# First-layer gating as one VectorE operation, (tanh + 1) x values, with its power of two moved behind it

## The chip, the cores and the metric

The kernel runs on one core of one Trainium2 chip, as one program on its five engines: TensorE (PE, with its weight loads as PEld), VectorE (DVE), ScalarE (ACT), GpSimd (POOL) and SyncE (SP), which issues the DMAs. The metric is the device time of one execution in microseconds (us), the median of several runs. Lower is better.

## The reference, cut to what matters

```python
def _attn_ref(q, k, v):                      # B, H, S, D = 4, 8, 576, 64
    scores = (1 / np.sqrt(D)) * np.matmul(q, k.transpose(0, 1, 3, 2))
    kth = np.partition(scores, -32, axis=-1)[..., -32:-31]
    scores = np.where(scores >= kth, scores, -1e9)
    attn = np.exp(scores - np.max(scores, axis=-1, keepdims=True))
    attn = attn / (np.sum(attn, axis=-1, keepdims=True) + 1e-9)
    return np.matmul(attn, v)

def _moe_ref(x, w_gate, w_val, w_out):       # 2304 tokens, 512 -> 1536 -> 512
    gate = 1.0 / (1.0 + np.exp(-(x @ w_gate)))
    return (gate * (x @ w_val) @ w_out)

def _moe2_ref(x, w_in, w_out):               # 512 -> 2048 -> 512
    r = np.maximum(x @ w_in, 0.0)
    return (r * r) @ w_out

# attention, then its heads laid side by side as (2304, 512), then _moe_ref, then _moe2_ref
```

The gate is a sigmoid, which the kernel computes as (tanh(z / 2) + 1) / 2. The change concerns the product of this gate with `x @ w_val`.

## The kernel before, in words

The 2304 tokens are 18 tiles of 128. They go through the kernel in 12 chunks (`CHUNKS`, line 29): chunks 0 to 5 are one tile each (N = 128 columns), chunks 6 to 11 two tiles each (N = 256). Attention runs ahead of the two dense layers, one row block (a tile and a head) at a time: scores by matmul (L376) copied to an SBUF tile `S` (L379), four rounds of MAX8 and three of MATCH_REPLACE8 on VectorE over that tile (L392, L399) for the 32nd largest score, exponentials on ScalarE (L411, L413 or L427), scaling on ScalarE and GpSimd, a transpose by matmul or DMA, and the product with the values.

The weights are first converted and then split into a high and a low float16 part (`split`, L663 on ScalarE, L666 on VectorE, L668 and L669 on GpSimd); that work lies before 377 us. Chunks 0 and 1 (`moe32`) go through the layers in float32 and are not touched by the change. Chunks 2 to 11 use the split weights and also split each activation into two float16 parts, so that a product takes three matmuls (high x high, high x low, low x high).

The first layer of a chunk from 2 on goes in six pairs of 128-wide blocks of the hidden dimension, `fp` = 0 to 5. For one pair, `l1_pair` in `moe_head` (L744 to L770):

- 24 matmuls fill the PSUM tile `pg` (gate) and 24 more the PSUM tile `pv` (values), both at L753. `pg`, `pv` and the second layer's `ph` share one pool of two PSUM buffers, so the `pv` of the next pair can begin only when the VectorE operation that reads this pair's `pv` is done.
- ScalarE takes the tanh of `pg` into the SBUF tile `th` (L763).
- GpSimd makes (th + 1) x 2^(-TB-1) of it in place (L764; TB is 15).
- VectorE multiplies `pv` and `th` into `th` (L765).
- ScalarE rounds `th` to float16, the high part `gh[:, 0]` (L768).
- GpSimd subtracts: the low part `gh[:, 1]` = th - gh[:, 0] (L769).

The tiles are `gh` here, and `gp` for the first two pairs of chunks 5 to 11, which `start` begins while the chunk before them still runs. `l1_acc` (L793) then multiplies both parts with the split `w_out` and sums in PSUM, one pair or two pairs behind. After pair 5, the sum is scaled and split for the second layer (L823 to L834), which runs through L858 (`ph`), L867 to L871 and L879, and the tile goes out at L897.

The order of the instructions on every engine is not written by hand. The Tile framework's scheduler plays the program in a timeline of its own and puts each instruction where it becomes ready there, under priorities: attention has a high priority and is emitted ahead of the layers (`attend`, `at`). Each engine then executes its own list strictly in order, and a wait at its head holds everything behind it. So an edit of one operation can move other instructions in all lists.

A split product's first two matmuls per PSUM bank need only the high part; the third row of each accumulation needs the low part.

Of the kernel before, what the change touches and what calls it, by code (L numbers as in the profile page):

```python
# [14 lines left out]
AF = mybir.ActivationFunctionType  # L15
ALU = mybir.AluOpType
# [53 lines left out]
TB = 15  # L70
# [3 lines left out]
def tile_topk_attention__then__two_moe_layers(  # L74
# [14 lines left out]
    nc = tc.nc  # L89
# [599 lines left out]
    def wblk(name, a, kt, f0, n):  # L689
        t, e = parts[(name, kt, f0 // 512)]  # L690
        return t[:, a, e, f0 % 512 : f0 % 512 + n]
# [42 lines left out]
    def moe_head(ci, x):  # L734
        m = ahead[ci] = Moe()
        m.gp, m.queue = None, []
        tts = chunks[ci]
        N = len(tts) * P
        ig = scales["wg"][1]
        xs, ix = x  # L740
        gsc = xsmall[ci].bitcast(F32)[:, 4:5]
        nc.vector.scalar_tensor_tensor(gsc, ix, 0.5, ig, op0=ALU.mult, op1=ALU.mult)

        def l1_pair(fp, gh=None):  # L744
            pg = ps_w.tile([P, 512], F32, tag="wk", name=f"pg_{ci}_{fp}")
            pv = ps_w.tile([P, 512], F32, tag="wk", name=f"pv_{ci}_{fp}")
            for pp, wd in ((pg, "wg"), (pv, "wv")):
                for e in range(2):
                    f0 = (2 * fp + e) * P
                    n = 0  # L750
                    for c in range(KM):
                        for a, b_ in SPLIT:
                            nc.tensor.matmul(  # L753
                                pp[:, e * N : (e + 1) * N],
                                wblk(wd, a, c, f0, P),
                                xs[:, b_, c, :],
                                start=(e == 0 and n == 0),
                                stop=(n == 3 * KM - 1),
                                skip_group_check=True,
                            )  # L760
                            n += 1
            th = mpool.tile([P, 2 * N], F32, tag="hi", bufs=HIB, name=f"th_{ci}_{fp}")
            nc.scalar.activation(th, pg[:, 0 : 2 * N], AF.Tanh, scale=gsc)  # L763
            nc.gpsimd.tensor_scalar(th, th, 1.0, float(2.0 ** (-TB - 1)), op0=ALU.add, op1=ALU.mult)  # L764
            nc.vector.tensor_tensor(th, pv[:, 0 : 2 * N], th, op=ALU.mult)  # L765
            if gh is None:
                gh = mpool.tile([P, 2, 2 * N], F16, tag="hi", bufs=HIB, name=f"gh_{ci}_{fp}")
            nc.scalar.copy(gh[:, 0], th)  # L768
            nc.gpsimd.tensor_tensor(gh[:, 1], th, gh[:, 0], op=ALU.subtract)  # L769
            return gh  # L770

        m.N, m.ix, m.l1_pair = N, ix, l1_pair
# [517 lines left out]
```

## Time and profile before

| What | Value |
|---|---|
| Time, median of 3 runs | 1262.53 us (1261.23 to 1262.6) |
| Profiled execution, first to last instruction (span) | 1261.3 us |
| PE busy | 1176.1 us, 93% of the span, 11477 matmuls |
| PE weight loads | 957.5 us, 76% |
| VectorE busy | 954.8 us, 76% |
| GpSimd busy | 846.5 us, 67% |
| ScalarE busy | 828.6 us, 66% |
| Chain that ended last | PE 67%, ACT 9%, POOL 7%, DVE 7%, DMA 5%, issue 3% |

The three runs are the record of the time; the profiled execution is recorded by its span alone, 1.2 us under their median. Busy time on PE includes matmuls whose ends are modelled, so a stretch with 100% is one in which PE always had a matmul under way. An idle engine costs nothing unless the end waits for it: what matters is where PE stood still, and who released it.

### The profile page before, as it was taken

What the parts mean: (1) busy time and instruction counts of PE and PEld (TensorE: products, weight loads), DVE (VectorE), ACT (ScalarE), POOL (GpSimd) and SP (SyncE); (2) the same over time, 40 slices, a digit from 0 to 9 for tenths busy, and PEclk for the clock granted to TensorE, in tenths of its full rate; (3) what the DMA queues carried; (4) which work ended last, traced back from release to release, by engine and by line L of the source; (5) the groups of instructions that cost most, each with busy time, mean ns of one, the idle gap of its engine ahead of it and who ended that gap; (6) DMA issues with size and microseconds to landing.
All of it is one profiled execution on the core that took longest, in us unless ns stands there. A gap on an engine that the chain in (4) does not pass through costs nothing.

```text
span 1261.3 us, 30690 instructions
## 1 busy us (share of the span) xinstructions
PE 1176.1 (93%) x11477; PEld 957.5 (76%) x11477; DVE 954.8 (76%) x1965; ACT 828.6 (66%) x1719; POOL 846.5 (67%) x1294
## 2 busy tenths in 40 slices
PE   6757989999889998899998999999999999999998
PEld 5536877987777877779787778877876887787775
DVE  6998789899977978899988899999789969110010
ACT  4998996577767676677776777776567657322122
POOL 1788774488876577797876987797678659425223
PEclk9986999999989999999999999999999999999999
DMA  7988762223344356665776575567434523200000
GB/s 188 366 298 275 260 199 81 59 76 90 113 131 130 81 125 159 143 136 130 137 157 133 125 181 115 127 140 158 77 73 97 116 54 60 53 2 1 17 1 18
DMA packets 243190, 153.94 MB, mean 122 GB/s; under 512 B 193120, under 2 KB 209504, under 8 KB 243040
## 3 DMA queue, kind: packets, MB, share of 16 engines
q1 hardware_dynamic: 243040, 151.97, 47.7%
q8 instruction: 91, 1.49, 0.5%
q14 instruction: 59, 0.48, 0.1%
HBM read 105.51 MB, written 18.09 MB: 98 GB/s over the span
## 4 chain that ended last, share of the span: by engine, by line
PE 67%; ACT 9%; POOL 7%; DVE 7%; DMA 5%; issue 3%; SPq 2%; POOLq 0%; ACTq 0%; DVEq 0%
PE ph L858 12%; PE acc L879 12%; PE acc L793 8%; PE pg L753 8%; PE pv L753 8%; PE sp L376 5%; PE xp L509 3%; DMA PT<-S 3%; DVE mx L392 2%; PE xp L536 2%; DVE W L399 2%; PE pg L912 1%; PE qpt L336 1%; PE ph L959 1%; PE acc L976 1%
## 5 line engine op out<-in xcount | busy, mean ns | idle before, releaser
L392 DVE MAX8 mx<-W 128x8 f32<-128x576 f32 x432 | 327.9, 759 | 11.2
L399 DVE MATCH_REPLACE8 W<-mx,W 128x576 f32<-128x576 f32 x288 | 213.8, 742 | 0.0
L858 PE MATMUL ph<-x,wi_w 128*128 128x256 f16 (+1 forms) x1920 | 190.9, 253 | 2.7 <-ACT x L832 2.6
L879 PE MATMUL acc<-w_w,rh 128*128 128x512 f16 x768 | 182.2, 379 | 0.9 <-POOL rh L871 0.9
L858 PEld LDWEIGHTS <-wi_w 128*128 128x128 f16 x1920 | 156.4, 99 | 29.0 <-issue 4.0
L753 PE MATMUL pg<-xs,wg_w 128*128 128x256 f16 (+1 forms) x1440 | 148.4, 254 | 1.1 <-ACT th L763 0.8
L753 PE MATMUL pv<-xs,wv_w 128*128 128x256 f16 (+1 forms) x1440 | 143.8, 252 | 5.1 <-DVE th L765 3.7
L376 PE MATMUL sp<-kst,qt 128*128 128x288 f32 x608 | 132.9, 330 | 6.5 <-ACT rh L869 2.5
L457 POOL TENSOR_TENSOR S<-W,S 128x512 f16<-128x512 f32 x192 | 137.0, 735 | 2.1
L379 ACT COPY S<-sp 128x576 f32<-128x576 f32 x144 | 91.8, 638 | 66.3 <-PE sp L376 39.7
L793 PEld LDWEIGHTS <-wo_w 128*128 128x128 f16 x1440 | 119.6, 99 | 19.2 <-issue 7.4
L411 ACT ACTIVATE W<-S,mx 128x576 f32<-128x576 f32 x144 | 111.8, 776 | 30.9 <-DVE mx L392 30.5
L753 PEld LDWEIGHTS <-wg_w 128*128 128x128 f16 x1440 | 118.9, 99 | 17.2 <-issue 1.4
L753 PEld LDWEIGHTS <-wv_w 128*128 128x128 f16 x1440 | 117.4, 98 | 18.1 <-issue 5.8
L765 DVE TENSOR_TENSOR th<-pv,th 128x512 f32<-128x512 f32 (+1 forms) x60 | 34.7, 579 | 125.4 <-PE pv L753 121.0
L879 PEld LDWEIGHTS <-rh 128*128 128x128 f16 x768 | 72.0, 98 | 73.3 <-POOL rh L871 1.2
L392 DVE MAX8 mx<-S 128x8 f32<-128x576 f32 x144 | 107.3, 745 | 25.9 <-ACT S L379 24.1
L793 PE MATMUL acc<-gh,wo_w 128*128 128x256 f16 (+1 forms) x1104 | 105.6, 250 | 4.7 <-ACT gh L768 2.6
L399 DVE MATCH_REPLACE8 W<-mx,S 128x576 f32<-128x576 f32 x144 | 106.9, 742 | 0.0
L455 POOL TENSOR_SCALAR W<-W,bs 128x576 f32<-128x576 f32 x96 | 71.6, 746 | 52.6 <-ACT S L454 47.8
L870 POOL TENSOR_TENSOR r<-r 128x512 f32<-128x512 f32 (+1 forms) x80 | 69.6, 869 | 54.8 <-ACT rh L869 54.1
L376 PEld LDWEIGHTS sp<-kst,qt 128*128 128x128 f32 x608 | 90.8, 192 | 17.5 <-issue 3.8
(246 smaller groups left out, 2331.5 us busy)
## 6 DMA issues: line engine op xcount, KB each, us to landing
kst<-ks SPq DMA_DIRECT2D x112, 288.0 KB, 3.1
v<-vd SPq DMA_DIRECT2D x32, 320.0 KB, 3.3
qn<-in_q_dram SPq DMA_DIRECT2D x128, 64.0 KB, 2.3
wi_r<-in_moe_w_in_dram SPq DMA_DIRECT2D x16, 512.0 KB, 6.2
w_r<-in_moe_w_out_dram SPq DMA_DIRECT2D x16, 512.0 KB, 4.5
v<-in_v_dram SPq DMA_DIRECT2D x56, 128.0 KB, 2.4
wg_r<-in_moe_w_gate_dram SPq DMA_DIRECT2D x12, 512.0 KB, 6.0
wv_r<-in_moe_w_val_dram SPq DMA_DIRECT2D x12, 512.0 KB, 7.3
```

What stands on the lines that cost most here:

```text
L376: nc.tensor.matmul(sp[:, e, 0:HALF], l, r, start=(x == 0), stop=(x == len(ops) - 1))
L379: nc.scalar.copy(ss.rearrange("p (e s) -> p e s", e=2), sp[:, :, 0:HALF])
L392: m8 = nc.vector.max(mx[:, min(r, 1)], cur)
L399: nc.vector.match_replace(wk, mx[:, min(r, 1)], cur, NEG)
L411: nc.scalar.activation(wk, ss, AF.Prelu, bias=kth, scale=-1.0, alpha=1.0 / BIG)
L455: nc.gpsimd.tensor_scalar(wk, wk, rz, 1.0, op0=ALU.mult, op1=ALU.mult)
L457: nc.gpsimd.tensor_tensor(pp[:, o : o + e - f], wk[:, f:e], pp[:, f:e], op=ALU.subtract)
L753: nc.tensor.matmul(pp[:, e * N : (e + 1) * N], wblk(wd, a, c, f0, P), xs[:, b_, c, :], start=(e == 0 and n == 0), stop=(n == 3 * KM - 1), ...
L793: nc.tensor.matmul(accs[d // 2][:, (d % 2) * N : (d % 2 + 1) * N], wblk("wo", a, f, d * P, P), gh[:, b_, e * N : (e + 1) * N], start=(f == ...
L858: nc.tensor.matmul(ph[:, e * N : (e + 1) * N], wblk("wi", a, c, f0, P), x2[:, b_, c, :], start=(e == 0 and n == 0), stop=(n == 3 * KM - 1) ...
L870: nc.gpsimd.tensor_tensor(r, r, r, op=ALU.mult)
L879: nc.tensor.matmul(acc2[i][:, 0:DM], gh[:, b_, e * N + i * P : e * N + (i + 1) * P], wblk("w2", a, f, 0, DM), start=(f == 0 and x == 0), s ...
```

## The change

The factor 2^(-16) leaves the gate and goes behind the product. VectorE computes (th + 1) x pv in one operation, straight from the tanh. ScalarE's copy to float16 takes the factor as its scale, and GpSimd multiplies the float32 product by the same factor, in place, before it subtracts.

```diff
             th = mpool.tile([P, 2 * N], F32, tag="hi", bufs=HIB, name=f"th_{ci}_{fp}")
             nc.scalar.activation(th, pg[:, 0 : 2 * N], AF.Tanh, scale=gsc)
-            nc.gpsimd.tensor_scalar(th, th, 1.0, float(2.0 ** (-TB - 1)), op0=ALU.add, op1=ALU.mult)
-            nc.vector.tensor_tensor(th, pv[:, 0 : 2 * N], th, op=ALU.mult)
+            nc.vector.scalar_tensor_tensor(
+                th, th, 1.0, pv[:, 0 : 2 * N], op0=ALU.add, op1=ALU.mult
+            )
             if gh is None:
                 gh = mpool.tile([P, 2, 2 * N], F16, tag="hi", bufs=HIB, name=f"gh_{ci}_{fp}")
-            nc.scalar.copy(gh[:, 0], th)
+            nc.scalar.activation(gh[:, 0], th, AF.Copy, scale=float(2.0 ** (-TB - 1)))
+            nc.gpsimd.tensor_scalar(th, th, float(2.0 ** (-TB - 1)), 1.0, op0=ALU.mult, op1=ALU.mult)
             nc.gpsimd.tensor_tensor(gh[:, 1], th, gh[:, 0], op=ALU.subtract)
             return gh
```

In the changed kernel the VectorE operation is L764, the copy L769, the GpSimd multiplication L770 and the subtraction L771; every later line is two higher. The same number of operations is issued on each engine. Up to the first gating of chunk 2 the lists are the same; from there on they differ in many places. Three of them, all in chunk 2, follow. In a name such as `th_2_5_4241` the first number is the chunk, the second the pair, the last a buffer; `mx`, `W` and `S` tiles belong to attention (tile, then head), `w2_w` and `wi_w` to the weight split, and `x_3s`, `xt_3` and `xs_3` to the input of chunk 3.

VectorE, around the gating of pair 2 of chunk 2, before:

```order
L392 MAX mx_4_2_3821<-W_4_2_3820 128x8
L742 SCALAR_TENSOR_TENSOR x_3s_3573<-x_3s_3573,wsmall_89 128x1
L399 MATCH_REPLACE W_4_2_3820<-mx_4_2_3821,W_4_2_3820 128x576
L666 SCALAR_TENSOR_TENSOR w2_w4_3284<-w2_c4_1698,wsmall_89,w2_w4_3284 128x1024
L392 MAX mx_4_2_3821<-W_4_2_3820 128x8
L765 TENSOR_TENSOR th_2_2_3914<-pv_2_2_3865,th_2_2_3914 128x256
L392 MAX mx_4_3_4052<-S_4_3_3763 128x8
```

The same place in the changed kernel:

```order
L392 MAX mx_4_2_3821<-W_4_2_3820 128x8
L742 SCALAR_TENSOR_TENSOR x_3s_3573<-x_3s_3573,wsmall_89 128x1
L764 SCALAR_TENSOR_TENSOR th_2_2_3914<-th_2_2_3914,pv_2_2_3865 128x256
L399 MATCH_REPLACE W_4_2_3820<-mx_4_2_3821,W_4_2_3820 128x576
L666 SCALAR_TENSOR_TENSOR w2_w4_3284<-w2_c4_1698,wsmall_89,w2_w4_3284 128x1024
L392 MAX mx_4_2_3821<-W_4_2_3820 128x8
L764 SCALAR_TENSOR_TENSOR th_2_3_3995<-th_2_3_3995,pv_2_3_3946 128x256
```

The gating of pair 2 stands three large operations earlier, right behind L742, and that of pair 3 now comes before the first MAX of the next row block.

GpSimd, at the same pair, with what each instruction waits for, before:

```order
L224 TENSOR_TENSOR voe_1_0_3384<-ve_1_0_3380,voe_1_0_3384 64x2x64 [waits Pool_49]
L764 TENSOR_SCALAR th_2_2_3914<-th_2_2_3914 128x256 [waits Activation_49]
L716 TENSOR_SCALAR xt_3_2931<-xt_3_2931,x_3s_3573 128x512 [waits Activation_49]
L717 TENSOR_TENSOR xs_3_3566<-xt_3_2931,xs_3_3566 128x512 [waits PE_49,Pool_49]
L408 TENSOR_SCALAR bs_4_1_3694<-mx_4_1_3668 128x1
```

In the changed kernel:

```order
L224 TENSOR_TENSOR voe_1_0_3384<-ve_1_0_3380,voe_1_0_3384 64x2x64 [waits Pool_49]
L716 TENSOR_SCALAR xt_3_2931<-xt_3_2931,x_3s_3573 128x512 [waits Activation_49]
L770 TENSOR_SCALAR th_2_2_3914<-th_2_2_3914 128x256 [waits Activation_49]
L717 TENSOR_TENSOR xs_3_3566<-xt_3_2931,xs_3_3566 128x512 [waits PE_49,Pool_49]
L771 TENSOR_TENSOR gh_2_2_3917<-th_2_2_3914,gh_2_2_3917 128x256 [waits PE_49,Pool_49]
```

GpSimd's multiplication still waits for ScalarE, but now for the copy L769, which reads the tile that it overwrites; the subtraction behind it waits for GpSimd's own result and no longer for ScalarE.

GpSimd, at the last pair of chunk 2, before:

```order
L764 TENSOR_SCALAR th_2_5_4241<-th_2_5_4241 128x256 [waits Activation_49]
L408 TENSOR_SCALAR bs_4_4_4318<-mx_4_4_4310 128x1 [waits DVE_49]
L431 TENSOR_SCALAR bs_4_3_4078<-bs_4_3_4078 128x1 [waits Activation_49]
L220 MEMSET voe_1_2_4009 64x2x64 [waits DMAHW6_49,DMAHW4_49,Pool_49]
L431 TENSOR_SCALAR bs_4_4_4318<-bs_4_4_4318 128x1 [waits Activation_49,Pool_49]
L769 TENSOR_TENSOR gh_2_5_4245<-th_2_5_4241,gh_2_5_4245 128x256 [waits Activation_49]
```

In the changed kernel:

```order
L668 TENSOR_SCALAR w2_c6_1722<-w2_c6_1722,wsmall_89 128x1024 [waits Activation_49]
L770 TENSOR_SCALAR th_2_5_4241<-th_2_5_4241 128x256 [waits Activation_49]
L669 TENSOR_TENSOR w2_w6_3450<-w2_c6_1722,w2_w6_3450 128x1024 [waits Pool_49]
L771 TENSOR_TENSOR gh_2_5_4244<-th_2_5_4241,gh_2_5_4244 128x256 [waits PE_49,Pool_49]
L408 TENSOR_SCALAR bs_4_3_4078<-mx_4_3_4052 128x1
```

The four attention operations that stood between the two gating steps of this pair now stand behind them, and one of the weight split stands between. In PE's list, 24 matmuls lie between the last one of this pair's `pv` and the first that reads its `gh` before the change, and 56 after it.

## Rows read from the trace of the kernel before

**Rows 1.** Stretches, all engines: us, busy us (instructions) per engine, clock, DMA share, GB/s.

```profile
300.00:376.00 76.00, 66.87 (x795) 58.94 (x795) 67.01 (x134) 55.98 (x126) 59.20 (x90) 0.93 0.42 119
376.00:700.00 324.00, 303.81 (x3817) 257.01 (x3815) 282.37 (x631) 229.98 (x538) 237.76 (x435) 0.99 0.59 132
700.00:1090.00 390.00, 389.99 (x3719) 303.63 (x3714) 336.19 (x695) 265.37 (x551) 299.69 (x489) 1.00 0.52 110
```

**Rows 2.** Waits of PE, 300 to 700 us: us in total, times, longest.

```profile
PE kpt L164 <- DMA kn<-in_k_dram: 5.5, 3, 2.8
PE pv L753 <- DVE th L765: 3.7, 1, 3.7
PE acc L793 <- ACT gh L768: 2.6, 1, 2.6
PE sp L376 <- ACT rh L869: 2.5, 1, 2.5
...
PE acc L793 <- POOL gh L769: 2.0, 2, 1.6
```

**Rows 3.** Timeline of PE, chunk 2: start, us, operation, idle before and releaser.

```profile
335.24 1.50 PE L753 MATMUL pg<-xs,wg_w 128*128 128x128 f16 x24
340.45 2.06 PE L753 MATMUL pv<-xs,wv_w 128*128 128x128 f16 x24 [3.70 <-DVE th L765]
...
342.58 2.46 PE L753 MATMUL pg<-xs,wg_w 128*128 128x128 f16 x24
...
363.68 2.29 PE L793 MATMUL acc<-gh,wo_w 128*128 128x128 f16 x20 [1.55 <-POOL gh L769]
```

**Rows 4.** Stretches before and behind two stalls of PE, columns as in group 1.

```profile
335.00:340.40 5.40, 1.74 (x32) 1.62 (x30) 5.40 (x7) 1.37 (x2) 4.72 (x7) 1.00 0.29 70
340.40:345.00 4.60, 4.55 (x53) 4.53 (x53) 3.83 (x7) 4.60 (x14) 4.36 (x6) 0.63 0.04 9
361.50:366.00 4.50, 2.69 (x25) 2.53 (x25) 3.73 (x10) 1.18 (x5) 2.80 (x7) 0.52 0.59 145
```

**Rows 5.** Timeline of VectorE around the gating of pair 2, chunk 2.

```profile
334.32 2.20 DVE L742 SCALAR_TENSOR_TENSOR x_3s<-x_3s,wsmall 128x1 f32<-128x1 f32 x1
...
337.17 2.23 DVE L666 SCALAR_TENSOR_TENSOR w_w<-w_c,wsmall,w_w 128x1024 f16<-128x1024 f32 x1
339.32 0.75 DVE L392 MAX8 mx<-W 128x8 f32<-128x576 f32 x1
339.99 0.40 DVE L765 TENSOR_TENSOR th<-pv,th 128x256 f32<-128x256 f32 x1
```

**Rows 6.** Timeline of GpSimd, the same place.

```profile
336.00 0.40 POOL L764 TENSOR_SCALAR th<-th 128x256 f32<-128x256 f32 x1
...
337.17 1.15 POOL L717 TENSOR_TENSOR xs<-xt,xs 128x512 f16<-128x512 f32 x1
```

**Rows 7.** Groups by shape: busy us, mean ns of one, idle before.

```profile
L765 DVE TENSOR_TENSOR th<-pv,th 128x512 f32<-128x512 f32 x36 | 24.7, 687 | 121.9 <-PE pv L753 120.1 <-POOL th L764 1.2 <-POOL W L455 0.4
L833 DVE SCALAR_TENSOR_TENSOR x<-acc,x2s,x 128x512 f16<-128x512 f32 x12 | 8.6, 743 | 0.7 <-ACT x L832 0.6
L768 ACT CAST gh<-th 128x256 f16<-128x256 f32 x22 | 8.9, 406 | 2.8 <-DVE th L765 2.7
L869 ACT ACTIVATE rh<-r 128x256 f16<-128x256 f32 x32 | 13.4, 418 | 6.7 <-PE acc L879 3.2 <-POOL rh L871 3.1
L764 POOL TENSOR_SCALAR th<-th 128x256 f32<-128x256 f32 x24 | 9.7, 403 | 7.5 <-ACT th L763 7.5
L769 POOL TENSOR_TENSOR gh<-th,gh 128x256 f16<-128x256 f32 x22 | 15.1, 686 | 4.3 <-ACT gh L768 3.7
```

**Rows 8.** Timeline at the last pair of the last chunk.

```profile
1203.30 6.93 PE L793 MATMUL acc<-gh,wo_w 128*128 128x256 f16 x62
1203.57 0.69 DVE L765 TENSOR_TENSOR th<-pv,th 128x512 f32<-128x512 f32 x1 [7.17 <-PE pv L753]
...
1204.99 1.16 POOL L769 TENSOR_TENSOR gh<-th,gh 128x512 f16<-128x512 f32 x1 [2.72 <-ACT gh L768]
```

## The prediction

> **What bounds the kernel now.** I read four views, in this order. The stretches come first [rows 1]. From 700 to 1090 us PE is busy 389.99 of 390 us: there it is the bound, and nothing that happens on another engine can show in the time. From 376 to 700 us PE is busy 303.81 of 324 us (20.2 us idle) while VectorE is busy 282.37; from 300 to 376 us it is 66.87 of 76 (9.1 us idle), at a granted clock of 0.93. The kernel's matmuls are the same before and after, so the end moves by what PE's idle time before 700 us changes, and by what its clock loses there. Behind that the two layers of the last chunks are alone on PE; I come to their last gating below.
>
> The second view is who released PE between 300 and 700 us [rows 2]. Three of the lines belong to the gating: `pv` waits 3.7 us for VectorE's product L765, and `l1_acc` waits 2.6 us for ScalarE's copy L768 and 2.0 us for GpSimd's subtraction L769. They sum to 8.3 us. The timeline of PE [rows 3] puts them all into chunk 2's first layer: 3.70 us before 340.45, and up to 363.68 the two waits for the last pair, where PE reached `gh` early because only 24 matmuls lay between.
>
> The third view is the clock behind those stalls [rows 4]. PE worked at a granted clock of 1.00 up to the first stall and at 0.63 in the 4.6 us behind it; behind the second pair of stalls it was 0.52, that is almost all at the lower of its levels, 1.2 GHz, and not at 2.4. So a stall is paid for twice: 24 matmuls took 2.06 and 2.46 us behind it against 1.50 before, and 20 took 2.29 us, where 20/24 of 1.50 is 1.25 [rows 3]. That is 0.56 + 0.96 + 1.04 = 2.6 us.
>
> The fourth view explains the 3.70 us. VectorE's list had the product of pair 2 behind L742, a MATCH_REPLACE8, the weight split L666 (2.23 us) and a MAX8 [rows 5]; it began at 339.99. Its GpSimd input was done at 336.4 [rows 6] because GpSimd, in order, had been busy with the split of the attention values until 336.0. The scheduler had put the product late for the sake of that input.
>
> **The change, part by part.** *The GpSimd step leaves the path to the product.* That input is gone. In the new list the product of pair 2 stands right behind L742, which ended near 336.5, so it can end near 336.9 and not at 340.4. The `pv` of pair 3 then follows the `pg` that ended near 336.75 (335.24 + 1.50) with almost no gap: nearly all of the 3.70 us goes. What is late next is the low part of pair 2. The copy L769 can run from 337.0 to 337.4, the GpSimd multiplication (0.40) ends near 337.85, but L717 (1.15) stands between it and the subtraction (0.69), so the low part is there near 339.7. PE, with `pv` done at about 338.35, now goes straight to that pair's `l1_acc` and waits 1.35 us. I keep 1.35.
>
> *The step comes back behind the copy.* The words "beside that copy" do not hold: the multiplication writes `th` in place, so it waits for ScalarE's copy, as its wait in the list shows. The chain from product to low part becomes product, copy, multiplication, subtraction: 0.42 + 0.42 + 0.40 + 0.69 = 1.9 us for the narrow chunks, against 1.5 before [rows 7]. PE covers it wherever more work than this lies between: the smallest distance in the new list from a `pv` to the first matmul on its `gh` is 36 matmuls (pair 5 of chunk 3), or about 36 x 1.50 / 24 = 2.25 us. For the last pair of chunk 2 the distance grows from 24 to 56, about 3.5 us or more, and the four attention operations, two with a wait for ScalarE, no longer stand in GpSimd's gap; instead L669 does. I take 0.75 us as left of the 4.2 us there, halfway between none and the 1.55 us of the old wait for the subtraction.
>
> From chunk 5 on two pairs are under way, no distance in the new list is below 48 matmuls, and from 700 us on PE is full, so the longer chain is free. At the very end the low part of the last pair was ready at 1206.15 [rows 8]; 0.6 us more leaves it at 1206.8. On PE two earlier `l1_acc` of 24 matmuls each stand in front: 62 took 6.93 us, so 48 last from 1203.3 to 1208.7 [rows 8]. Free, with 1.9 us to spare.
>
> *VectorE's operation changes form.* It reads one tensor from SBUF and one from PSUM, as before. The nearest row of the same form and sources is L833, 743 ns at 512 columns against 687 for L765 [rows 7]; the other bound is no change. I take the upper one: +56 ns each, and less for the narrow ones. Of the 60 instances, those of chunks 2 to 6 lie where PE is not yet full: 30, at most 1.7 us of VectorE time. VectorE is 87% busy there (282.37 of 324 us [rows 1]), so I charge 1.0 us. The Trainium skill, "VectorE: DVE Perf Modes" (section "Why PSUM operands drop a tier"), holds any float32 operation with a PSUM operand to one result per cycle and makes no difference by form; by it this 1.0 us would be 0, and no row here shows this form with a float32 result.
>
> *ScalarE's copy gets a scale.* The nearest row is L869, an activation with a constant scale from SBUF to float16: 418 ns at 256 columns against 406 [rows 7]. That is +12 ns, 60 times, 0.7 us on an engine that is a third idle: 0.
>
> *GpSimd's work* is the same two operations a pair. What changes is that its list no longer stops at the tanh, only at the copy; attention operations behind it come earlier. I count nothing for it. No DMA is added or removed, though the order of some on SyncE's queue shifts.
>
> **The sum.** Removed: 8.3 us of stalls and 2.6 us of slow clock. Left or added: 1.35 + 0.75 + 1.0. Net 10.9 - 3.1 = 7.8 us by the end of chunk 2's first layer. Not all of this reaches 700 us. If attention comes forward as well, all of it does. If not, PE runs dry later, since the 20.2 us of idle time from 376 to 700 us is spent on waits such as 5.5 us for key loads and 2.5 us for `rh` [rows 2], which earlier layer work does not shorten. Between 0 and 7.8 I take half, 3.9, since VectorE, which paces attention, was itself not idle in the first stall (5.40 of 5.40 us [rows 4]) but lost 0.8 us in each of the two slow stretches. Against the median of 1262.5 (the profiled span is 1261.3, so the sum is of one execution 1.2 us shorter) that gives 1258.6 us.
>
> **The rivals.** *It only moves the idle time.* The lists differ in many places from chunk 2 on, and the net 7.8 us is used up by later waits. For it: attention work keeps its pace, and the scores of the next row blocks stand later among the layer's matmuls. Against it: PE is saturated later, so idle time once saved need not return. Time 1262, chance 0.24.
>
> *The longer chain is exposed, and it ends slower.* In chunks 3 and 4 the first layer runs one pair deep, with 36 to 107 matmuls of cover. ScalarE or GpSimd operations that stand in between (as L717 did with 1.15 us, or an L666-sized one with 2.2) push the low part past PE's arrival. The decisive point is a delay of more than about 0.4 us at the tightest pair (2.25 less 1.9) and 1.6 us at 56 matmuls (the first pair of chunk 4). Three such stalls of 2 us, each with 1 us of slow clock behind it (the 2.6 us came from three stalls), cost 9 us; less half of the 7.8 this is +5. Against it: the old chain, only 0.4 us shorter, stalled PE in chunk 2 alone. Time 1267, chance 0.26.
>
> *The new lists are better throughout.* All of the 7.8 us reaches the end, and a wait of 2.5 us elsewhere goes too: 1252. That is inside the forecast's direction, chance 0.12 of the 0.50 that I give to faster.
>
> **How the numbers follow.** 0.2% is 2.5 us, about what a measurement of this kernel can tell from no change. Faster by more: 0.50 (the forecast and the better case). Within: 0.24. Slower by more: 0.26. The range has to hold both signs: below, 7.8 us and one wait of 2.8 [rows 2] give 1252; above, the slower rival's 1267. Some tail beyond each is left out. The forecast's own range is 1254 to 1260.
>
> **What would show it.** Right: in the waits of PE, the line of `pv` for the VectorE operation is under 1 us, and those of `acc` for ScalarE and GpSimd are together under 3; the clock of 300 to 376 us is above 0.95; L764 takes 690 to 745 ns, L769 about 628, L770 617 at 512 columns; PE's idle time from 300 to 700 us falls from 29.3 to about 25. Wrong: `acc` waits for L771 in chunks 3 or 4, or waits for key loads and transposes grow by what the gating gave up.

## The result, and the profile after

The changed kernel is slower: 1272.59 us as the median of four runs (1268.48 to 1275.72) against 1262.57 us for the kernel before beside it, a ratio of 1.0088 with an interval of 1.0064 to 1.0112. The medians differ by 10.0 us, and the ratio is worth 11, where 4 us less were forecast; 1272.6 lies above the range. The profiled execution took 1272.85 us (span 1271.1). Ratios here and below are not the quotients of the two medians, from which they differ by up to 0.14%.

From the page of the changed kernel, busy times and the chain that ended last:

```profile
PE 1177.3 (93%) x11477; PEld 956.5 (75%) x11477; DVE 950.7 (75%) x1965; ACT 828.9 (65%) x1719; POOL 844.7 (66%) x1294
...
PE 61%; POOL 9%; DVE 8%; ACT 8%; DMA 8%; issue 4%; SPq 3%; POOLq 0%; ACTq 0%; DVEq 0%
```

No engine has noticeably more to do than before: PE's busy time grew by 1.2 us, VectorE's fell by 4.1. PE's part of the chain fell from 67% to 61%; DMA (5% before), GpSimd (7%) and VectorE (7%) took most of that over. The stretches of [rows 1], in the changed kernel (us, busy us and instructions of PE, PEld, DVE, ACT, POOL, granted clock, DMA share, GB/s):

```profile
300.00:376.00 76.00, 66.45 (x792) 56.86 (x791) 63.47 (x133) 57.51 (x127) 59.49 (x92) 0.98 0.39 110
376.00:700.00 324.00, 302.32 (x3757) 253.59 (x3755) 276.34 (x618) 222.39 (x528) 228.86 (x422) 0.97 0.59 132
700.00:1090.00 390.00, 387.97 (x3692) 302.76 (x3689) 342.91 (x710) 270.51 (x557) 305.56 (x498) 1.00 0.49 109
```

Three things differ from [rows 1]. The clock of the first stretch rose from 0.93 to 0.98, as forecast. That of the second fell from 0.99 to 0.97, and VectorE did 6 us less in it. And from 700 us on, where PE had been busy 389.99 of 390 us, it now stands still for 2 us. Who released PE between 300 and 700 us, to be held against [rows 2]:

```profile
PE sp L376 <- DMA kst<-ks: 6.6, 5, 1.7
PE kpt L164 <- DMA kn<-in_k_dram: 5.9, 3, 2.7
PE vn L214 <- ACT vs L205: 3.5, 2, 3.1
PE acc L881 <- POOL rh L873: 3.1, 2, 2.5
PE acc L795 <- POOL gh L771: 2.7, 2, 1.8
PE x2pq L827 <- ACT x L825: 2.7, 2, 1.5
PE xp L509 <- DMA PT<-S: 2.0, 2, 1.5
```

The 3.7 us of `pv` for VectorE's product are gone, and so are the 2.6 us of `acc` for ScalarE's copy. In their place stand waits that have nothing to do with the gating: key loads (`kst`), value norms (`vn`), the second layer's `rh`. For the transfers, the kernel before had:

```profile
PE sp L376 <- DMA kst<-ks: 1.7, 2, 1.0
PE xp L509 <- DMA PT<-S: 1.2, 2, 0.7
```

The gating itself, by shape (count, then busy us, mean ns of one, idle time of the engine before them):

```profile
L764 DVE SCALAR_TENSOR_TENSOR th<-th,pv 128x512 f32<-128x512 f32 x36 | 24.5, 681 | 117.8 <-PE pv L753 116.0 <-ACT W L411 1.3 <-ACT S L379 0.4
L764 DVE SCALAR_TENSOR_TENSOR th<-th,pv 128x256 f32<-128x256 f32 x24 | 9.9, 414 | 12.3 <-ACT th L763 7.9 <-PE pv L753 2.2 <-POOL gh L771 1.7
L769 ACT ACTIVATE gh<-th 128x512 f16<-128x512 f32 x24 | 15.0, 627 | 29.2 <-DVE th L764 29.2
L770 POOL TENSOR_SCALAR th<-th 128x512 f32<-128x512 f32 x36 | 22.2, 618 | 95.5 <-ACT gh L769 63.0 <-ACT gp L769 32.1 <-ACT vs L205 0.2
```

VectorE's new form takes 681 ns where the old product took 687 [rows 7]. So no operation of the gating got slower by more than 17 ns (ScalarE's copy of 256 columns, 406 ns before and 423 now), and the loss is to be looked for in what the rest of the program does around them.

### The profile page after: what moved, and what is told of

Read it like the earlier page. It is cut to its first block, busy times and chain, and to the rows that moved or that the text cites. A ratio compares the mean times of both kernels' runs of the same rounds, so it can differ in the third digit from the quotient of the medians.

```text
span 1271.1 us, 30671 instructions
## 1 busy us (share of the span) xinstructions
PE 1177.3 (93%) x11477; PEld 956.5 (75%) x11477; DVE 950.7 (75%) x1965; ACT 828.9 (65%) x1719; POOL 844.7 (66%) x1294
## 4 chain that ended last, share of the span: by engine, by line
PE 61%; POOL 9%; DVE 8%; ACT 8%; DMA 8%; issue 4%; SPq 3%; POOLq 0%; ACTq 0%; DVEq 0%
PE ph L860 10%; PE acc L881 9%; PE pg L753 8%; PE acc L795 8%; PE pv L753 7%; PE sp L376 5%; DVE mx L392 3%; PE xp L509 3%; DVE W L399 3%; DMA PT<-S 2%; PE xp L536 2%; DMA kst<-ks 2%; PE pg L914 1%; POOL S L457 1%; PE acc L936 1%
## 5 line engine op out<-in xcount | busy, mean ns | idle before, releaser
L764 DVE SCALAR_TENSOR_TENSOR th<-th,pv 128x512 f32<-128x512 f32 (+1 forms) x60 | 34.5, 575 | 130.1 <-PE pv L753 118.2
L795 PEld LDWEIGHTS <-wo_w 128*128 128x128 f16 x1440 | 117.0, 98 | 16.3 <-issue 4.0
```

What stands on the lines that cost most here:

```text
L795: nc.tensor.matmul(accs[d // 2][:, (d % 2) * N : (d % 2 + 1) * N], wblk("wo", a, f, d * P, P), gh[:, b_, e * N : (e + 1) * N], start=(f == ...
```

## Two theories, and how they were told apart

**The lists.** The change makes the scheduler draw new lists (the order of the instructions on each engine) from chunk 2 on, and these make PE wait more. **The operations.** The chain product, copy, multiplication, subtraction is longer and is exposed somewhere (the rival at 1267).

They can be separated, because an engine's order can be held. At the end of the program every instruction of an engine is chained to the one that is to stand ahead of it, by a dependency that is to set the order and add no wait (shortened; `lists` stands for the stored orders):

```diff
         tile_topk_attention__then__two_moe_layers(tc, *args)
+        pin(tc, nc)
...
+def pin(tc, nc):
+    at = {i.name: i for i in nc.cur_bb.bb.instructions}
+    for wanted in lists:
+        for earlier, later in zip(wanted, wanted[1:]):
+            tc.add_manual_dep(at[later], at[earlier].name, NOSYNC, reason="order")
```

`lists` holds the names of one engine's instructions in the order of either kernel; VectorE's product, ScalarE's copy and GpSimd's subtraction have a counterpart in both. GpSimd's fourth step (L764 before, L770 after) has none and finds its own place. In e1's trace PE, VectorE, ScalarE and SyncE run everything but the gating in the order of the kernel before, without one difference, and so does GpSimd but for four instructions at the start. Every kernel below computes the whole of the reference. Ratios are against runs of the kernel before on the same chip, whose medians were 1261.5 to 1262.7 us.

| Run | Operations | Lists | Median us | Ratio [interval] |
|---|---|---|---|---|
| e1 | changed | of before | 1263.74 | 1.0014 [1.0002, 1.0026] |
| e2 | before | of the changed kernel | 1272.78 | 1.0075 [1.0055, 1.0096] |
| e3 | changed | of before, gating free | 1266.24 | 1.0032 [1.0018, 1.0045] |
| e4 | before | of before (9 units in the first layers) | 1262.59 | 1.0000 [0.9987, 1.0012] |
| e5 | changed | its own | 1272.16 | 1.0088 [1.0062, 1.0115] |
| e6 | changed | new to 404 us, then of before | 1265.32 | 1.0031 [1.0019, 1.0043] |
| e7 | changed | of before to 404 us, then new | 1270.93 | 1.0067 [1.0047, 1.0088] |
| e8 | changed | new, SyncE's of before | 1287.80 | 1.0203 [1.0190, 1.0216] |
| e9 | changed | new, seven key loads earlier | 1274.38 | 1.0102 [1.0085, 1.0120] |
| e10 | changed | its own (9 units in the first layers) | 1272.93 | 1.0080 [1.0058, 1.0102] |
| e11 | changed | drawn anew, 13 units in the later layers | 1271.41 | 1.0078 [1.0061, 1.0094] |
| e12 | before | drawn anew, 13 units in the later layers | 1269.98 | 1.0057 [1.0035, 1.0079] |
| e13 | changed | of before to 700 us, then new | 1267.13 | 1.0039 [1.0025, 1.0052] |
| e14 | changed | new to 700 us, then of before | 1270.41 | 1.0048 [1.0032, 1.0064] |
| e15 | before | drawn anew, 15 units in the later layers | 1267.94 | 1.0042 [1.0026, 1.0058] |
| e16 | changed | drawn anew, 15 units in the later layers | 1266.80 | 1.0037 [1.0019, 1.0055] |

## Operations against lists: e1, e2, e3

e1, the changed operations with `lists` of the kernel before:

> The changed operations (VectorE (tanh+1) x values, ScalarE copy with the power of two, GpSimd multiplication right ahead of its subtraction), while every other instruction of all five engines is held in the order that it has in the kernel before; the product, the copy and the subtraction keep the places that they had there. Theory 1 (the loss comes from the new lists: the scheduler put attention work, weight splits and SyncE's transfers in another order, and PE waits more for key loads): 1260 to 1266 us, the waits for key loads and transposes as before (sp for kst about 2 us between 300 and 700, not 6.6). Theory 2 (the loss comes from the changed operations themselves: the longer chain product, copy, multiplication, subtraction): 1269 to 1275 us, with acc waiting for GpSimd more than the 2.0 us of before.

e2, the operations of before with `lists` of the changed kernel:

> The reverse: the operations of the kernel before, while every other instruction of all five engines is held in the order that it has in the changed kernel; only GpSimd's first step of the gating finds its own place. Theory 1: 1269 to 1277 us, with sp waiting for kst 5 us or more between 300 and 700. Theory 2: 1260 to 1266 us.

Measured: 1263.74 and 1272.78. The changed operations in the old lists cost 0.14% (1.8 us); the old operations in the new lists cost 0.75% (9.5 us). The theory of the lists holds in both directions, and the longer chain is worth at most the 0.26% at the end of e1's interval. In e1 PE's waits for the gating changed names rather than length (300 to 700 us):

```profile
PE xp L509 <- DMA PT<-S: 4.3, 5, 1.3
PE acc L795 <- ACT gh L769: 3.8, 2, 2.7
PE acc L795 <- POOL gh L771: 3.5, 4, 1.5
PE pv L753 <- DVE th L764: 2.1, 1, 2.1
...
PE sp L376 <- DMA kst<-ks: 0.7, 1, 0.7
```

That is 9.4 us for the three gating lines against 8.3 before [rows 2], while the key loads stay short. The transposes do not: they held PE for 4.3 us, against 1.2 before, which theory 1 had not expected.

e3 leaves the four gating operations out of `lists`, so that they alone may move forward, which is what the prediction counted on:

> As the first of these, but the four operations of the gating behind the tanh (product, copy, multiplication, subtraction) may move in their engines' lists; all else stands as in the kernel before. Theory 1: 1255 to 1262 us, the 3.7 us wait of pv for the product in chunk 2 gone and nothing new in its place. Theory 2: 1267 to 1275 us.

Measured: 1266.24, worse than e1 (1263.74) and between the two ranges, above that of the lists and just below that of the operations. The product of pair 2 of chunk 2 did move, from 339.99 [rows 5] to 335.87, and the wait of `pv` was gone. But PE stopped for 4.59 us in the same place. VectorE, ScalarE, GpSimd and PE there (start, us, operation, idle before and releaser):

```profile
335.87 0.41 DVE L764 SCALAR_TENSOR_TENSOR th<-th,pv 128x256 f32<-128x256 f32 x1
...
336.93 3.26 DVE L666 SCALAR_TENSOR_TENSOR w_w<-w_c,wsmall,w_w 128x1024 f16<-128x1024 f32 x1
...
340.23 1.15 ACT L663 ACTIVATE wi_w<-wi_c,wsmall 128x1024 f16<-128x1024 f32 x1 [3.50 <-DVE w_w L666]
...
342.56 0.45 ACT L763 ACTIVATE th<-pg,x_2s 128x256 f32<-128x256 f32 x1
...
336.96 0.39 POOL L770 TENSOR_SCALAR th<-th 128x256 f32<-128x256 f32 x1
337.33 1.15 POOL L717 TENSOR_TENSOR xs<-xt,xs 128x512 f16<-128x512 f32 x1
338.45 0.66 POOL L771 TENSOR_TENSOR gh<-th,gh 128x256 f16<-128x256 f32 x1
339.10 1.27 POOL L408 TENSOR_SCALAR bs<-mx 128x1 f32<-128x1 f32 x1
...
343.07 2.72 PE L753 MATMUL pg<-xs,wg_w 128*128 128x128 f16 x24 [4.59 <-ACT th L763]
```

ScalarE's list has a copy of the weight split (L663) ahead of the next pair's tanh, and that copy waits for VectorE's split L666, which here took 3.26 us and 2.23 in [rows 5]. The `pg` of the pair behind waits for the buffer that this tanh reads. In the kernel before that tanh was done at 342.53, just ahead of the `pg` that began at 342.58 [rows 3]:

```profile
342.06 0.47 ACT L763 ACTIVATE th<-pg,x_2s 128x256 f32<-128x256 f32 x1
```

So the 3.7 us were never the product's alone: beside them stood a second chain, VectorE's split to ScalarE's copy to the tanh, that left no room.

## Is any new set of lists a loss? e4, e10, e11, e12, e15, e16

The scheduler was to draw anew without a change of any operation, by the number of units that attention runs ahead: 10 in the first layers (`LEAD`), 14 in the later ones (`LEAD2`).

```diff
-LEAD = 10
+LEAD = 9
```

> The kernel before with one number of the order changed (how many units attention runs ahead in the first layers, 9 and not 10): no operation differs, only the lists from chunk 2 on. Theory 1: such a change of the lists alone moves the time by 2.5 us or more, in either direction (1250 to 1260 or 1265 to 1275). Theory 2 says nothing of it but a change of the lists alone should matter little: 1260 to 1265.

> The changed kernel with attention 9 and not 10 units ahead in the first layers: the scheduler draws its lists anew for the same operations. If the loss is one unlucky set of lists, not a property of these operations: 1262 to 1268. If any lists that the scheduler makes for these operations lose: 1269 to 1276.

```diff
-LEAD2 = 14
+LEAD2 = 13
```

> The changed kernel with attention 13 and not 14 units ahead in the later layers. As for the run with 9: 1262 to 1268 if the lists were unlucky, 1269 to 1276 if any lists for these operations lose.

> The kernel before with 13 and not 14 units: no operation differs. If lists drawn anew cost some tenths of a per cent whatever the operations, since those of the kernel before are the best of several: 1265 to 1275. If its scheduler's lists are as good for any such number: 1260 to 1264.

```diff
-LEAD2 = 14
+LEAD2 = 15
```

> The kernel before with attention 15 and not 14 units ahead in the later layers; no operation differs. If the lists of the kernel before are a favourable draw among neighbours (13 units cost 0.57%): 1266 to 1275. If 13 was the exception: 1260 to 1264.

> The changed kernel with 15 and not 14 units. If the changed operations have some favourable set of lists near by, as the kernel before has with 14: 1258 to 1266. If they lose with every number near by (13 units gave 1271.4, 14 units 1272): 1268 to 1276.

The number for the first layers redrew nothing. In e4's trace VectorE, ScalarE, GpSimd and SyncE run the same lines on the same tiles and shapes in the same order as in the kernel before, from first to last, and PE differs in four matmuls near 36 us; e10 stands to the changed kernel in the same way. (Traces leave buffer numbers out, so that a swap of two operations alike in all this would not show.) So e4 and e10 are repeats, at 1262.59 and 1272.93, and say nothing about new lists; what e4's theory 1 expected of a redrawing was not put to the test by it. The number for the later layers does redraw: e12 leaves the lists of before at 592 us and e15 at 488, e11 and e16 leave those of the changed kernel at about 490.

With 13 units the old operations take 1269.98 and the changed ones 1271.41; with 15, 1267.94 and 1266.80. So at the two neighbouring numbers old and new operations differ by +0.21% (0.78 less 0.57, each uncertain by some 0.2) and -0.05%: nothing that these runs can tell from no change. Only at 14 do they differ by 0.88%. (e16 fell between its two expectations, with single runs from 1259.5 to 1272.4; e10 and e11 fell into the one of a loss. It is e12 and e15 that show that a loss does not need the changed operations.) The kernel before has favourable lists at that number, and each of the five other sets that were tried (the changed kernel's, e11, e12, e15, e16), whether its cause was a number or an operation, cost 0.37 to 0.88%. Five are few, and three of them share their first 490 us. With e1 and e2 that is the answer to why a change that removed its stalls came out slower.

## Where the new lists lose: e5 to e9, e13, e14

The changed kernel once more, unedited:

> The changed kernel once more, for a second profile. It is to show how much of the difference ahead of 316 us is its own: the lists are those of the kernel before up to there, yet its first profile stood 1.9 us later at the first matmul of chunk 2 and had 4.6 us more of idle PE. If that belongs to one execution, this profile stands within 0.5 us of the kernel before at that matmul and still ends at 1270 to 1274; if it belongs to the kernel, it is 1.5 us late again.

It ended at 1272.16, and its first matmul of chunk 2 came 2.9 us late, where the first profile had 1.9; both have lower clock around 175 us, but so has e11, which came 0.3 us late. Three others with new lists (e2, e9, e10) were within 0.4 us there and still took 1272.8 to 1274.4. That early loss is therefore not what makes the difference; what causes it in those two profiles stays open.

Four cuts change lists at one moment: every engine follows the one kernel's list up to it, and takes what is left in the order of the other.

> The changed operations; every list is held as in the changed kernel up to the end of chunk 2 (404 us) and behind that as in the kernel before. If the new lists gain in chunk 2 (its second layer begins 4 us earlier there) and lose only behind it: 1257 to 1262. If the gain in chunk 2 is attention's loss, to be paid later whatever follows: 1264 to 1270. If the changed operations cost what is lost: 1269 to 1275.

> The changed operations; every list as in the kernel before up to 404 us, and as in the changed kernel behind that. If the loss sits behind chunk 2: 1268 to 1274. If it sits in chunk 2: 1262 to 1266.

> The changed operations; every list as in the kernel before up to 700 us and as in the changed kernel behind that. The prediction held that from 700 us on nothing on another engine can show, since PE was busy 389.99 of 390 us there: then 1262 to 1265, like the changed operations in the lists of before (1263.7). If the new lists let PE run dry there by themselves: 1266 to 1271.

> The reverse cut: lists of the changed kernel up to 700 us, those of the kernel before behind that. If the loss is made by 700 us, as attention's delay of 10 us at row block 88 says, and is only collected later: 1269 to 1274. If it is made behind 700 us: 1263 to 1267.

Of the runs with changed operations, e1 has none of the new lists (0.14%). New lists up to 404 us bring e6 to 0.31%, from 404 to 700 as well e14 to 0.48%; behind 700 us alone they bring e13 to 0.39%. So the three pieces cost 0.17, 0.17 and 0.25%, with the operations 0.73% in sum (9.2 us) against 0.88 measured for the whole. Each difference is uncertain by about 0.2%, so that only the last is clear of zero, and the pieces cannot be ranked: by medians the second is the largest (4.2 us, against 1.4 and 2.3). e7 gives the lists behind 404 us directly: 0.67 less 0.14, or 0.53%. For e6 and e7 the second and the first expectation held (1264 to 1270, 1268 to 1274). The cut at 700 us was to tell on which side of it the loss is made, and both sides came out with one: 1267.13 is in e13's range for PE running dry by itself, 1270.41 in e14's for a loss made by 700 us. So neither side has all of it.

The loss can be followed in attention's progress, one row block (tile and head) after the other. Start of the first MAX8 of a block, and how much later it starts in the other profiles (us):

```
block  before     e1     e6    e13     e9  after    e12
   40   390.5    0.7    0.5    0.0    1.3    1.9   -1.0
   56   499.7    1.9    2.3   -0.5    3.0    7.1   -0.8
   72   604.6    2.9    2.9    1.5    6.2   10.0    0.4
   88   712.2    3.5    3.1    6.5   11.9   12.9    3.0
  104   812.9    4.3    3.8    9.8   14.4   15.7    9.4
  112   858.7    4.1    3.6   12.5   17.5   17.9   11.5
  143  1070.9    3.8    3.5    5.1    8.7    9.5    6.0
```

In the changed kernel attention falls 18 us behind, and about half of that is left at the end. e6 shows that what chunk 2 gains does not last: its second layer began 5.8 us earlier than before, and by chunk 3's second layer it was 1.7 us late. Presumably the first layer had gone ahead of attention's matmuls, which then had to be made up. e12 shows the same fall behind with no operation changed, and late: from block 72 on, as its lists change only at 592 us. Delay and loss do not go in step, though: at block 112 e16 is 14.4 us late and e15 2.1, and their last chunks begin 5.0 and 2.1 us late. That attention's delay is the cause is not shown; no run moves attention alone.

In e13 all lists are old up to 700 us, and still PE runs dry behind that, by its waits from 700 to 930 us and the stretch (columns as above):

```profile
PE xp L509 <- DMA PT<-S: 1.7, 2, 1.1
PE sp L376 <- DMA kst<-ks: 1.0, 1, 1.0
```

```profile
700.00:930.00 230.00, 227.17 (x2240) 179.38 (x2239) 201.74 (x424) 157.89 (x336) 177.34 (x302) 1.00 0.58 126
```

In the kernel before PE was busy 229.99 us of these 230. So with other lists a late transpose or key load stopped PE even in its fullest stretch.

Whether SyncE's transfers do it was tried twice. e8 takes `lists` of the changed kernel for four engines and that of the kernel before for SyncE:

> The changed operations and the changed kernel's lists on PE, VectorE, ScalarE and GpSimd; only SyncE's list of transfers is that of the kernel before. If the loss comes from the place of the key loads in SyncE's list (kst behind the stores of value pieces): the waits of sp for kst fall from 6.6 us to under 3 and the time to 1263 to 1267. If the order on the compute engines sets when keys can be loaded: the waits stay or move to other loads, 1270 to 1276.

1287.8 us, far above both expectations, with 12.5 us of waits for `kst` from 300 us on. SyncE's old list, which serves the old lists of the others, does not fit these new ones. e9 moves only seven key loads, each ahead of the transpose behind which the new list had put it. The place of one of them, SyncE's queue in the changed kernel:

```profile
476.42 1.32 SPq L459 DMA_TRANSPOSE PT<-S  x1
...
481.46 2.10 SPq L328 DMA_DIRECT2D kst<-ks  x2
```

and in e9:

```profile
470.25 0.62 SPq L328 DMA_DIRECT2D kst<-ks  x1
473.08 1.32 SPq L459 DMA_TRANSPOSE PT<-S  x1
```

> The changed kernel with its own lists but for one thing: in SyncE's list seven of the 112 key loads (kst), which stand there behind one transpose more than in the kernel before, stand ahead of that transpose again. If key loads behind a transpose that waits for attention are what carries the loss: the waits of sp for kst fall from 7 to 8 us to under 4, attention's row block 56 starts 2 us or more earlier, and the time is 1263 to 1268. If they are only one of many places at which the new lists wait: 1268 to 1273.

The local effect came: waits of `sp` for `kst` between 300 and 700 us fell from 6.6 to 3.6 us, and block 56 started 3.0 us late, not 7.1. The time did not follow (1274.38). By block 88 attention was 11.9 us late again. That fits the second expectation, by which key loads behind transposes are one of many places, although the time lies above its range too.

PE's side of the account, by stretches in the kernel before:

```profile
316.00:404.00 88.00, 78.75 (x1015) 67.72 (x1014) 72.17 (x149) 62.79 (x147) 66.46 (x110) 0.94 0.44 122
404.00:700.00 296.00, 275.92 (x3489) 235.80 (x3487) 262.34 (x589) 210.60 (x489) 217.80 (x395) 0.99 0.60 133
700.00:930.00 230.00, 229.99 (x2267) 182.69 (x2262) 205.70 (x431) 160.60 (x341) 179.14 (x303) 1.00 0.58 127
```

and in the changed kernel:

```profile
316.00:404.00 88.00, 77.88 (x998) 65.55 (x998) 67.90 (x148) 63.60 (x149) 66.67 (x112) 0.98 0.43 122
404.00:700.00 296.00, 274.89 (x3442) 232.99 (x3443) 256.89 (x577) 203.70 (x480) 208.90 (x383) 0.97 0.59 131
700.00:930.00 230.00, 227.97 (x2249) 180.23 (x2247) 204.76 (x429) 162.18 (x343) 182.53 (x309) 1.00 0.56 127
```

PE's idle time grows by 0.87, 1.03 and 2.02 us, 3.9 in sum. As an estimate, the clock takes (1 - clock) x length: 5.3 us before and 1.8 after in the first stretch, 3.0 and 8.9 in the second, net 2.4 us, uncertain by some 2 since the clock has two digits. That accounts for 6.3 of the 7.9 us by which the first profile fell back between chunk 2's first matmul and the last chunk's (1.9 to 9.8 us late). The second profile of the same kernel, e5, divides the loss otherwise:

```profile
316.00:404.00 88.00, 78.40 (x976) 65.72 (x976) 67.94 (x147) 63.98 (x148) 67.84 (x113) 0.94 0.44 120
404.00:700.00 296.00, 276.20 (x3487) 234.14 (x3485) 260.08 (x584) 206.83 (x484) 211.27 (x386) 0.98 0.59 132
700.00:930.00 230.00, 224.79 (x2186) 176.70 (x2185) 200.40 (x416) 156.78 (x332) 178.41 (x300) 0.99 0.57 126
```

There PE's idle time grows by 0.35, -0.28 and 5.20 us, and the clock by the same estimate takes 0, 3.0 and 2.3 us more: 10.5 us, where this profile fell back by 10.0 (2.9 to 12.9 us late). So the clock gave back in chunk 2 what the forecast said (3.5 us against 2.6) in one profile and nothing in the other. What both share is a loss behind 404 us, by this estimate 9 to 10 us of idle time and slow clock together.

## Why the prediction was wrong, point by point

*The removed stalls: right.* The wait of `pv` was to fall under 1 us and fell to 0; those of `acc` for ScalarE and GpSimd were to be under 3 us in sum and were 2.7; the clock from 300 to 376 us was to be above 0.95 and was 0.98. In e5, the second profile, the stalls are gone too, but that clock was 0.93, as before the change.

*PE's idle time: wrong.* From 300 to 700 us it was to fall from 29.3 to about 25 us, and rose to 31.2 (29.4 in e5). The sign named for a wrong prediction came instead: waits for key loads and transposes grew by 5.7 us (1.7 to 6.6 and 1.2 to 2.0), about the 5.6 that the gating gave up (8.3 to 2.7).

*What is left of the gating: right in kind, off in size.* PE at the two places in the changed kernel and behind the second, and GpSimd between multiplication and subtraction of either pair:

```profile
340.94 1.22 PE L795 MATMUL acc<-gh,wo_w 128*128 128x128 f16 x19 [0.92 <-POOL gh L771]
...
360.23 1.39 PE L795 MATMUL acc<-gh,wo_w 128*128 128x128 f16 x22 [1.81 <-POOL gh L771]
363.16 0.55 PE L827 MATMUL x2pq<-x,ones 128*128 128x128 bf16 x4 [1.55 <-ACT x L825]
366.80 0.19 PE L214 MATMUL vn<-vs,ones 128*128 128x1 bf16 x2 [3.10 <-ACT vs L205]
...
338.14 2.12 POOL L717 TENSOR_TENSOR xs<-xt,xs 128x512 f16<-128x512 f32 x1
...
357.42 2.13 POOL L669 TENSOR_TENSOR w_w<-w_c,w_w 128x1024 f16<-128x1024 f32 x1
```

The low part of pair 2 cost 0.92 us (1.35 predicted), that of the last pair 1.81 (0.75). L717 was taken as 1.15 us and took 2.12; at the last pair the 56 matmuls counted between `pv` and `gh` did not cover a chain with L669's 2.13 us in it. Two new stalls of 1.55 and 3.10 us follow at once. Even so, chunk 2's second layer began 4.0 us earlier than before, 5.9 us better than at its first matmul; 7.8 was predicted. e2, with the old operations, has 4.3 there: this gain too is one of the lists, not of the operation.

*VectorE's form: the wrong bound was taken.* +56 ns were taken from L833; measured were 681 against 687 ns, below the 690 to 745 foretold. The Trainium skill, "VectorE: DVE Perf Modes" (section "Why PSUM operands drop a tier"), by which the 1.0 us charged for it would be 0, agrees with the trace here.

*ScalarE's scale and GpSimd's multiplication: right.* 627 ns for the copy (about 628 predicted) and 618 for the multiplication (617).

*The longer chain behind chunk 2 and at the end: right.* PE never waited for L771 in chunks 3 and 4, and no loss arose from chunk 9 on, where the delay stays near 9.8 us.

*The step that failed* is the last of the sum: "Between 0 and 7.8 I take half, 3.9". It took 0 as the worst that the rest of the new lists could do, and the part on GpSimd had said "I count nothing for it" of attention operations that move and of the order on SyncE's queue. The runs show a loss there instead: the lists behind 404 us cost 0.42% by the cuts (0.17 + 0.25) and 0.53% by e7 less e1, some 5 to 7 us, and the gain was gone at chunk 3's second layer, 8.2 us late in the changed kernel. The rival of idle time that only moves (1262) named the mechanism, later waits, but priced it at no loss; the slower rival (1267) had the sign, but by the longer chain, which e1 bounds at 0.26%. The list of signs that would prove it wrong held the right one, with no price on it.

*A second step failed with it*: that from 700 us on "nothing that happens on another engine can show". PE's full stretch [rows 1] was a property of the old lists. With new ones behind 700 us alone, e13 lost 0.25% more than e1.

## What to carry to other kernels

Where a scheduler orders the engines, an edit can be two changes, the operation and a new set of lists, and a kernel with a favourable set can lose some tenths of a per cent with another (here 0.37 to 0.88%, against 0.14% for the operations). Before a stall is priced as a gain, redraw the lists by a neutral number to see the spread, see in the trace that they did change (here one of the two numbers changed nothing), and to judge the operation hold the old order. One profile is also not the kernel: two of the same one placed the loss differently. And ask of each stall which second chain ends just behind it: when the product moved up by 4 us, PE waited 4.59 us for a tanh instead of 3.70 for the product.

## What the runs showed of the hardware that was not expected

The same VectorE split takes very different times. For one weight, L666 in e3 (min/median/max ns, first and last start in us):

```profile
L666 DVE SCALAR_TENSOR_TENSOR w_w<-w_c,wsmall,w_w x5: 1277/1565/3261, 320.5 to 361.5; 128x1024 f16<-128x1024 f32 x5
```

The 3.26 us fell on the stretch shown for e3, in which GpSimd worked without a gap from 336.96 to 340.37. The Trainium skill, "GPSIMD Engine Reference" (section "Specifications"), says that GpSimd shares its SBUF interfaces with VectorE, with contention for VectorE instructions of two SBUF inputs, as this one is. The trace fits it, but no run isolates it. One split in the kernel before kept its 1.27 us beside a GpSimd subtraction, which began 0.02 us behind it:

```profile
275.28 1.27 DVE L666 SCALAR_TENSOR_TENSOR wg_w<-wg_c,wsmall,wg_w 128x1024 f16<-128x1024 f32 x1
275.30 1.84 POOL L352 TENSOR_TENSOR qt<-qn,qt 128x256 fp32r<-128x256 f32 x1
```

There it was GpSimd that lost: its 64 subtractions of this shape average 0.76 us. So either engine can be the one that is slowed. That the earlier gating steps on GpSimd are what slowed the split in e3 is not shown.
